# One transpose moved from DMA to TensorE, and one mask copy split and moved, in a block-sparse attention + gated MLP kernel

## The chip, the cores and the metric

The kernel runs on one core of a Trainium2 chip. A core has five engines that run at the same time, each with its own instruction queue: TensorE (PE, matrix products; its weight loads are listed as PEld), VectorE (DVE), ScalarE (ACT), GpSimd (POOL) and SyncE (SP), which here issues DMA transfers. The metric is the device time of one execution in microseconds (us).

## The reference

Inputs are q, k and v of shape (4, 8, 768, 64): batch, heads, sequence, head size. The first half is attention under a block mask with blocks of 32 positions; the second is a gated MLP over the 512 features of all heads.

```python
scores = scale * np.matmul(q, k.transpose(0, 1, 3, 2))
mask = np.abs(blk_i - blk_j) <= 1                      # neighbours
mask = mask | first and last block row and column      # edges
mask[qb block, kb block] = True for kb in sampled_blocks[qb]   # 3 per block row
attn = softmax(np.where(mask, scores, -1e9))
x = (attn @ v), heads side by side                     # (4, 768, 512)

h = np.maximum(x @ w_in, 0.0)                          # (4, 768, 1024)
u, v = h[..., :512], h[..., 512:]
v_n = (v - mean(v)) / np.sqrt(var(v) + 1e-06)
v_s = np.einsum('ts,bsd->btd', w_spatial, v_n) + b_spatial[None, :, None]
out = (u * v_s) @ w_out                                # (4, 768, 512)
```

(The mask and softmax lines are told in words here; the rest is the reference's.)

## The kernel before

**Layout.** A sequence of 768 positions is 6 chunks of 128 (`NCH`). Heads go in pairs; `p` from 0 to 15 counts pairs over all batches, four per batch. The big tile `kq` holds, for each of the 8 heads of a batch, 88 partitions: 64 with the transposed keys or queries, and 24 (`MR`, one per block) with mask rows. In the key half the mask rows say which block a position is in; in the query half they hold a penalty for each block, computed once for head 0 by `mask_rows` and the same for every head. A score product over all 88 partitions so adds the mask by itself. The rows of head 0 must therefore be copied to heads 1 to 7 once, and that is what `rows(hs, cs, eng)` does (line 239, its copies at lines 242 and 244): to heads `hs`, columns `cs`. `qcols(t, n)` names `n` thirds of the query columns from third `t` on; a third (`TW`) is 256 columns.

**First batch.** While inputs arrive, batch 0 is computed in units of a head pair and a third of the queries: first pair 0, then the pairs 1 to 3 for the first third, then the pairs 1 to 3 for the second third, then all four for the last. A unit is three slots of score products (`qk_unit`, line 405), each followed by one ScalarE exponential (line 410), and some slots later three slots of products with the values (`av_unit`, line 451), the last with a normalization on VectorE (lines 433 and 434). Units start at slots 0, 3, 6, and so on: unit 4 (pair 3, first third) at slot 12, unit 5 (pair 1, second third) at slot 15, unit 6 (pair 2, second third) at slot 18.

**Slots.** The main loop goes through numbered slots. In each it issues a score product, value products, then whatever `when(slot, ...)` has listed for it, in the order of listing. The list `ROWS` lists the mask copies; they are listed ahead of the transposes `tr_rest`. `tr_first(p)` and `tr_rest(p)` transpose a pair's keys and queries on TensorE (line 267) into a PSUM bank, from which VectorE copies them into `kq` (line 214). `tr_first` of pair 3 is in slot 10, `tr_rest` of pairs 1, 2, 3 and 0 in slots 8, 11, 14 and 17. These banks come from two that take turns (`moe_tag`), which the MLP products use too. The waits between engines follow from what each instruction reads and writes.

**GpSimd** casts what arrives from HBM to bf16, in the order in which the casts are written out: of the keys, queries and values of the pairs 0 to 3 (line 134), and then the pieces of `w_in` (line 230). SP issues the loads in its own written order; a load waits until its staging buffer is free.

**Later batches** run with whole heads (`qk_full`, line 418, exponential at line 422, `av_full`, line 469), and the MLP of the batch before (class `Moe`, products at line 545) is dealt out between them, a few products a slot.

**The last batch's MLP** has no attention beside it. Its steps are `s_product(0..5)`, the spatial product of each chunk, and then `o_product(0..5)`, the output product. The end of an `s_product` is one VectorE instruction at line 613, which writes the gated chunk into `un`. The output product needs it transposed, in `gt`, and gets it by `dma_start_transpose` on SP's queue (line 623): two chunks at a time, but chunks 4 and 5 of the last batch each by itself. Output chunks leave PSUM by ScalarE (even) or VectorE (odd), lines 217 and 214, and are written to HBM by SP (line 642); the last chunk is done in two halves of 256 columns, the second of which goes out on ScalarE's queue. PSUM banks of the last batch's products come in turn from three pairs of banks: `moe`, `av` and `sc` (`moe_ps`).

Of the kernel before, what the change touches and what calls it, by code (L numbers as in the profile page):

```python
# [26 lines left out]
def kernel(  # L27
# [22 lines left out]
    NCH = S // 128  # L50
# [5 lines left out]
    NDH = DH // 128  # L56
# [29 lines left out]
    K_, Q_ = slice(0, S), slice(S, 2 * S)  # L86

    def qcols(t0, n=1):
        return slice(S + t0 * TW, S + (t0 + n) * TW)
# [4 lines left out]
    def dram(src, p, hs=slice(0, 2), cs=slice(0, NCH)):  # L94
        b, g = divmod(p, NG)
        return src[b, 2 * g + hs.start:2 * g + hs.stop].rearrange(
            "h (p c) d -> p h (c d)", c=NCH)[:, :, cs.start * D:cs.stop * D]
# [5 lines left out]
    def load(p, nm, hs=BOTH, cs=ALLC, eng=nc.sync):  # L103
        if (nm, p) not in st:
            st[nm, p] = work.tile([128, 2, S // 2], FP32, tag="st_" + nm, bufs=3, name="st_" + nm)
        eng.dma_start(out=st[nm, p][:, hs, cs.start * D:cs.stop * D],
                      in_=dram(SRC[nm], p, hs, cs))
# [4 lines left out]
    def nat0_view():  # L112
        return nat[0].rearrange("p c h d -> p (c h d)").rearrange("p (h x) -> p h x", h=2)

    def cast(p, nm, eng, hs=BOTH, cs=ALLC):
        if nm == "v":
            dst = vv[p % NVV][:, hs, cs, 0:D]
        else:
            if p not in nat:
                nat[p] = work.tile([128, 2 * NCH, 2, D], BF16, tag="nat", bufs=4, name="nat")  # L120
            c0 = 0 if nm == "k" else NCH
            dst = nat[p][:, c0 + cs.start:c0 + cs.stop].rearrange("p c h d -> p h c d")[:, hs]
        src = st[nm, p].rearrange("p h (c d) -> p h c d", d=D)[:, hs, cs]
        if p == 0 and nm != "v":
            dst = nat0_view()[:, hs, (c0 + cs.start) * D:(c0 + cs.stop) * D]
            if cs is not C45:
                dst = dst[:, 0].rearrange("p (i t d) -> p t i d", t=2, d=D)
                src = src[:, 0].rearrange("p (t i) d -> p t i d", t=2)
            else:
                dst = dst.rearrange("p h (c d) -> p h c d", d=D)  # L130
        if eng is nc.scalar:
            nc.scalar.activation(out=dst, in_=src, func=AF.Copy)
        else:
            eng.tensor_copy(out=dst, in_=src)  # L134
# [76 lines left out]
    PL, DV = nc.gpsimd, nc.vector  # L211

    def dve_copy(o, i):
        nc.vector.tensor_copy(out=o, in_=i)  # L214
# [24 lines left out]
    def rows(hs, cs, eng=nc.vector):  # L239
        src = kq[MR, 0:1, cs].to_broadcast([NB, hs.stop - hs.start, cs.stop - cs.start])  # L240
        if eng is nc.scalar:
            nc.scalar.activation(out=kq[MR, hs, cs], in_=src, func=AF.Copy)
        else:
            eng.tensor_copy(out=kq[MR, hs, cs], in_=src)  # L244
# [12 lines left out]
    def moe_tag():  # L257
        moe_tags.rotate(1)
        if moe_tags[0] in held:
            moe_tags.rotate(1)  # L260
        return moe_tags[0]

    def bank(nm="ps", tag=None):
        return psum.tile([128, 1024], BF16, tag=tag or moe_tag(), bufs=2 if tag else 1, name=nm)

    def tr(ps, c, in_):
        nc.tensor.transpose(out=ps[:, c * 128:(c + 1) * 128], in_=in_, identity=ident)  # L267
# [47 lines left out]
    load(3, "q")  # L315
    cast(3, "k", PL)
    cast(3, "q", PL)
    load(2, "v")
    load(0, "q", cs=C45)
    load(3, "v")  # L320
# [217 lines left out]
    def product(n, lhs, rhs, last, done, w=512):  # L538
        ref = {}
        out = []  # L540
        for i in range(n):
            def run(i=i):
                if i == 0:
                    ref["ps"] = moe_ps(last)
                nc.tensor.matmul(out=ref["ps"][:, 0:w], lhsT=lhs(i), rhs=rhs(i),  # L545
                                 start=(i == 0), stop=(i == n - 1))
                if i == n - 1:
                    done(ref["ps"][:, 0:w])
            out.append(run)
        return out  # L550
# [4 lines left out]
    class Moe:  # L555
# [55 lines left out]
        def s_product(self, tcc):  # L611
            def done(ps):
                nc.vector.scalar_tensor_tensor(out=self.un[:, tcc, :], in0=ps,  # L613
                                               scalar=b_col[:, tcc:tcc + 1],
                                               in1=self.un[:, tcc, :], op0=ALU.add,
                                               op1=ALU.mult)
                if self.last and tcc >= NCH - 2:
                    g0 = tcc
                elif tcc % 2 == 1:
                    g0 = tcc - 1  # L620
                else:
                    return
                nc.sync.dma_start_transpose(
                    out=self.gt[:, g0:tcc + 1].rearrange("p t c n -> p (t c) n"),
                    in_=self.un[:, g0:tcc + 1, :].rearrange("p t d -> p (t d)"))
            return product(NCH, lambda s: w_spt[:, tcc, s, :], lambda s: self.vn[:, s, :],
                           self.last, done)

        def o_product(self, tcc):
            steps = []  # L630
            osb = {}
            parts = 2 if self.last and tcc == NCH - 1 else 1
            w = DM // parts
            for i in range(parts):
                cs = slice(i * w, (i + 1) * w)

                def done(ps, i=i, cs=cs):
                    if i == 0:
                        osb["t"] = work.tile([128, DM], FP32, tag="osb", bufs=6, name="osb")
                    on_act = (tcc + i) % 2 == 0  # L640
                    (act_copy if on_act else dve_copy)(osb["t"][:, cs], ps)
                    (nc.scalar if i else nc.sync).dma_start(
                        out=out[self.b].rearrange("(p c) d -> c p d", c=NCH)[tcc][:, cs],
                        in_=osb["t"][:, cs])
                steps += product(NDH, lambda d: self.gt[:, tcc, d, :],
                                 lambda d, cs=cs: w_out_t[:, d, cs], self.last, done, w)
            return steps
# [7 lines left out]
        def rest_steps(self):  # L655
            out = []
            for tcc in range(NCH):
                out += self.s_product(tcc)
            first = out[0]
            out[0] = lambda: ([self.vn_one(True) for _ in range(NCH)], first())  # L660
            for tcc in range(NCH):
                out += self.o_product(tcc)
            return out

    queue = deque()
# [20 lines left out]
    def when(slot, *fns):  # L686
        at.setdefault(slot, []).extend(fns)

    def c(f, *a, **kw):
        return lambda: f(*a, **kw)  # L690

    K_Q0 = slice(0, S + TW)
    ROWS = [(1, 2, 8, qcols(0)), (1, 3, 4, K_), (5, 4, 6, K_), (6, 6, 8, K_), (9, 2, 8, qcols(1, 2))]
    when(0, second)
    when(1, third)
    when(2, lambda: filler(FILL3, psum.tile([128, 512], FP32, tag=moe_tag(), bufs=1, name="wps")))
    for p, sl in ((1, 4), (2, 7), (3, 10)):
        when(sl, c(tr_first, p))
    for sl, h0, h1, cs in ROWS:
        when(sl, c(rows, slice(h0, h1), cs))  # L700
# [146 lines left out]
```

## Time and profile before

| what | before |
|---|---|
| median of 3 runs | 216.38 us (216.07, 216.38, 217.03) |
| the profiled execution | 215.56 us, of which 213.8 us span from the first to the last instruction |
| mean granted TensorE clock | 0.999 of full speed |
| TensorE busy | 205.5 us (96%) |
| ScalarE busy | 170.6 us (80%) |
| VectorE busy | 132.9 us (62%) |
| GpSimd busy | 72.1 us (34%) |
| DMA | 41.83 MB, mean 196 GB/s |

The span is from one profiled execution, and every time inside it (a start, a duration, a wait) counts from the start of that span. In a timeline a row reads: start, duration, engine, line, operation, what is written `<-` what is read, shape, how many in a row, and in square brackets how long the engine stood idle before it and what ended that. In a chain a row reads: start, duration, engine, tile and line. Matmuls overlap in the pipeline, so a row of several takes less than the sum of their durations.

### The profile page before, as it was taken

Reading aid. Unit: us, or ns where it says so; the run is one execution under the profiler, and the core shown is the slowest. Engines: PE = TensorE matmul, PEld = TensorE weight load, DVE = VectorE, ACT = ScalarE, POOL = GpSimd, SP = SyncE. Lnnn points to the kernel's source line nnn. Section 1 sums busy time; section 2 is a strip of 40 time slices with the busy share of each in tenths; the row PEclk is TensorE's granted clock in tenths of the full one; section 3 lists DMA queues with packets and bytes.
Section 4 is the critical chain, followed back from the end, with each engine's and each line's share of the span. In section 5 each row is a group of like instructions: output and inputs, shape, how many; then the busy total and the mean of one; then the engine's idle time right before and its main releaser. Section 6 shows DMA issues by size and latency. Waiting matters only on the chain.

```text
span 213.8 us, 5290 instructions
## 1 busy us (share of the span) xinstructions
PE 205.5 (96%) x2147; PEld 130.2 (61%) x2147; DVE 132.9 (62%) x286; ACT 170.6 (80%) x226; POOL 72.1 (34%) x118
## 2 busy tenths in 40 slices
PE   8897999999999999999999999999999999999991
PEld 7686878766666666656556655665565565544431
DVE  7899585979554534494986454385874443486540
ACT  6997999999999999979998888979989776275021
POOL 6886669885681412223351040131020000022000
PEclk9999999999999999999999999999999999999999
DMA  5998899999999989899491597894101225500266
GB/s 155 351 373 307 257 339 284 274 229 326 277 362 193 259 268 256 267 308 212 112 224 37 62 316 154 217 317 85 37 3 37 49 52 135 220 29 0 51 148 247
DMA packets 63324, 41.83 MB, mean 196 GB/s; under 512 B 45124, under 2 KB 58052, under 8 KB 63300
## 3 DMA queue, kind: packets, MB, share of 16 engines
q1 hardware_dynamic: 62868, 41.11, 73.9%
q10 hardware_dynamic: 432, 0.39, 0.6%
q8 instruction: 17, 0.28, 0.5%
q14 instruction: 7, 0.06, 0.1%
HBM read 24.38 MB, written 6.29 MB: 143 GB/s over the span
## 4 chain that ended last, share of the span: by engine, by line
PE 89%; DVE 6%; DMA 2%; ACT 1%; issue 0%; DVEq 0%; ACTq 0%
PE ps_moe L545 33%; PE ps L418 22%; PE ps_av L469 13%; PE ps_t L545 6%; PE ps L405 5%; PE ps_av L451 3%; PE ps_sc L545 3%; DVE kq L214 3%; DVE kq L244 2%; DMA gt<-un 2%; PE wps L182 2%; PE ps_av L267 1%; DVE xn L434 1%; ACT osb L217 0%; PE ps L267 0%
## 5 line engine op out<-in xcount | busy, mean ns | idle before, releaser
L422 ACT ACTIVATE a_all<-ps 128x768 bf16<-128x768 f32 x144 | 113.9, 812 | 15.1 <-PE ps L418 7.6
L418 PE MATMUL ps<-kq 88*128 88x384 bf16 x288 | 70.5, 325 | 0.1
L469 PEld LDWEIGHTS <-a_all 128*128 128x128 bf16 x864 | 46.5, 97 | 20.0
L469 PE MATMUL ps_av<-vv,a_all 128*128 128x65 bf16 x864 | 51.2, 194 | 0.0
L418 PEld LDWEIGHTS <-kq 88*128 88x128 bf16 x288 | 28.0, 98 | 31.0 <-issue 0.9
L545 PE MATMUL ps_moe<-w_in_t,xt 128*128 128x512 bf16 x144 | 44.0, 378 | 0.1
L410 ACT ACTIVATE a_all<-ps 128x1024 bf16<-128x1024 f32 x36 | 34.8, 1026 | 2.8 <-PE ps L405 2.6
L545 PE MATMUL ps_moe<-vn,w_spt 128*128 128x512 bf16 x108 | 32.7, 378 | 0.0
L134 POOL CAST nat<-st_k 128x768 bf16<-128x768 f32 (+2 forms) x17 | 13.5, 796 | 42.6 <-DMA st_k<-in_k_dram 42.4
L433 DVE RECIPROCAL rc<-ps_av 128x6 f32<-128x6 f32 (+1 forms) x36 | 6.6, 184 | 29.3 <-PE ps_av L469 27.8
L405 PE MATMUL ps<-kq 88*128 88x256 bf16 (+1 forms) x140 | 21.5, 275 | 2.3 <-DVE kq L214 1.5
L582 POOL TENSOR_SCALAR std<-mv 128x3 f32<-128x3 f32 (+1 forms) x9 | 2.1, 238 | 63.6 <-DVE mv L579 47.5
L613 DVE SCALAR_TENSOR_TENSOR un<-ps_moe,b_col,un 128x512 bf16<-128x512 f32 x18 | 13.5, 749 | 16.2 <-PE ps_moe L545 15.7
L545 PE MATMUL ps_moe<-w_out_t,gt 128*128 128x512 bf16 x72 | 21.5, 378 | 0.0
L545 PEld LDWEIGHTS <-xt 128*128 128x128 bf16 x192 | 15.4, 97 | 7.3 <-issue 0.3
L434 DVE TENSOR_TENSOR xn<-ps_av,rc 128x384 bf16<-128x384 f32 (+1 forms) x36 | 18.5, 513 | 1.2
L578 DVE BATCH_NORM_STATS2 stats<-vn 128x6 f32<-128x512 bf16 x24 | 16.5, 687 | 1.4 <-ACT vn L573 0.9
L405 PEld LDWEIGHTS <-kq 88*128 88x128 bf16 x140 | 12.6, 97 | 6.2 <-DVE kq L214 2.3
L134 POOL CAST nat<-st_q 128x768 bf16<-128x768 f32 (+1 forms) x18 | 14.1, 782 | 5.9 <-DMA st_q<-in_q_dram 5.3
L214 DVE COPY kq<-tt 64x1536 bf16<-64x1536 bf16 x24 | 15.9, 660 | 0.3
L134 POOL CAST vv<-st_v 128x768 bf16<-128x768 f32 x16 | 13.8, 863 | 5.6 <-DMA st_v<-in_v_dram 5.5
L451 PE MATMUL ps_av<-vv,a_all 128*128 128x65 bf16 x288 | 14.8, 194 | 0.0
(81 smaller groups left out, 209.8 us busy)
## 6 DMA issues: line engine op xcount, KB each, us to landing
st_v<-in_v_dram SPq DMA_DIRECT2D x16, 384.0 KB, 5.8
out_dram<-osb SPq DMA_DIRECT2D x23, 256.0 KB, 3.1
st_k<-in_k_dram SPq DMA_DIRECT2D x15, 384.0 KB, 4.5
st_q<-in_q_dram SPq DMA_DIRECT2D x15, 384.0 KB, 5.1
ws_f<-in_moe_w_spatial_dram SPq DMA_DIRECT2D x6, 384.0 KB, 7.2
w_f<-in_moe_w_in_dram SPq DMA_DIRECT2D x8, 256.0 KB, 7.2
w_f<-in_moe_w_out_dram SPq DMA_DIRECT2D x4, 256.0 KB, 4.2
st_q<-in_q_dram SPq DMA_DIRECT2D x2, 128.0 KB, 4.8
```

The lines of the kernel that those rows point to most:

```text
L134: eng.tensor_copy(out=dst, in_=src)
L214: nc.vector.tensor_copy(out=o, in_=i)
L405: nc.tensor.matmul(out=ps[:, at:at + n * TW], lhsT=kq[:, h, ci * 128:(ci + 1) * 128], rhs=kq[:, h, qcols(t0, n)], start=True, stop=True)
L410: nc.scalar.activation(out=out, in_=ps, func=AF.Exp, scale=0.125)
L418: nc.tensor.matmul(out=ps[:, hf * 512:hf * 512 + HALF], lhsT=kq[:, j % H, ci * 128:(ci + 1) * 128], rhs=kq[:, j % H, S + hf * HALF:S + (hf ...
L422: nc.scalar.activation(out=a_ref["h", j][:, ci, :].rearrange("p (b c) -> p b c", b=2), in_=ps.rearrange("p (b c) -> p b c", b=2)[:, :, 0:H ...
L434: nc.vector.tensor_tensor(out=out, in0=ps[:, :, 0:D], in1=rc[:, 0:n].to_broadcast([128, n, D]), op=ALU.mult)
L451: nc.tensor.matmul(out=av_ref[u][:, to, :], lhsT=a_ref[u][:, at:at + 128], rhs=vv[pp % NVV][:, h, ci, :], start=(ci == 0), stop=(ci == NCH ...
L469: nc.tensor.matmul(out=av_ref[j][:, qc, :], lhsT=a_ref["h", j][:, ci, qc * 128:(qc + 1) * 128], rhs=vv[p % NVV][:, h, ci, :], start=(ci == ...
L545: nc.tensor.matmul(out=ref["ps"][:, 0:w], lhsT=lhs(i), rhs=rhs(i), start=(i == 0), stop=(i == n - 1))
L578: nc.vector.bn_stats(out=stats, in_=self.vn[:, tcc, :])
L613: nc.vector.scalar_tensor_tensor(out=self.un[:, tcc, :], in0=ps, scalar=b_col[:, tcc:tcc + 1], in1=self.un[:, tcc, :], op0=ALU.add, op1=AL ...
```

## The change

Three edits.

1. The mask rows of the second and third query third (`qcols(1, 2)`, 512 columns) of heads 2 to 7 were copied in slot 9 by VectorE in one instruction. Now heads 4 to 7 are copied by VectorE in slot 14, and
2. heads 2 and 3 by GpSimd, in its written-out sequence right after the casts of pair 3's keys and queries.
3. Chunk 5 of the last batch, the last gated one, is no longer transposed by DMA. A step put behind `o_product(1)` transposes its four 128x128 pieces on TensorE into a PSUM bank of the `av` pair, and VectorE copies them to `gt`.

```diff
     cast(3, "k", PL)
     cast(3, "q", PL)
+    rows(slice(2, 4), qcols(1, 2), PL)
     load(2, "v")
...
-                if self.last and tcc >= NCH - 2:
+                if self.last and tcc == NCH - 1:
+                    return
+                if self.last and tcc == NCH - 2:
                     g0 = tcc
                 elif tcc % 2 == 1:
                     g0 = tcc - 1
...
+        def g_transpose(self):
+            ps = bank("ps_g", "av")
+            for d in range(NDH):
+                tr(ps, d, self.un[:, NCH - 1, d * 128:(d + 1) * 128])
+            dve_copy(self.gt[:, NCH - 1].rearrange("p c n -> p (c n)"), ps[:, 0:NDH * 128])
...
             for tcc in range(NCH):
                 out += self.o_product(tcc)
+                if self.last and tcc == 1:
+                    out.append(self.g_transpose)
             return out
...
-    ROWS = [(1, 2, 8, qcols(0)), (1, 3, 4, K_), (5, 4, 6, K_), (6, 6, 8, K_), (9, 2, 8, qcols(1, 2))]
+    ROWS = [(1, 2, 8, qcols(0)), (1, 3, 4, K_), (5, 4, 6, K_), (6, 6, 8, K_), (14, 4, 8, qcols(1, 2))]
```

## The prediction

> **What bounds the kernel now.** I read the page first: its shares, then the chain that ended last, then that chain in two windows, then the timelines of the engines there.
>
> ```profile
> PE 205.5 (96%) x2147; PEld 130.2 (61%) x2147; DVE 132.9 (62%) x286; ACT 170.6 (80%) x226; POOL 72.1 (34%) x118
> ```
>
> TensorE (PE) is busy 96% of 213.8 us, so time can only come out of its few holes or its own work. The chain of waits gives two holes. In order of time, from 15 us:
>
> ```profile
> 15.46 0.43 DVE kq L214
> 15.89 0.03 issue
> 15.92 1.43 DVE kq L244
> 17.35 0.03 issue
> 17.38 0.19 DVE rc L433
> 17.58 0.02 issue
> 17.60 0.42 DVE xn L434
> 18.02 0.60 DVE kq L214
> 18.62 0.05 issue
> 18.67 0.61 PE ps L405 x4
> ```
>
> From 7.46 to 18.62 us the chain runs on VectorE alone. Line 244 at 15.92 is the slot-9 mask copy. Around it the timeline shows the price on the other engines:
>
> ```profile
> 15.71 0.83 POOL L134 CAST vv<-st_v 128x768 bf16<-128x768 f32 x1 [0.27 <-DMA st_v<-in_v_dram]
> 15.99 0.61 PE L267 MATMUL ps<-ident,nat 128*128 128x128 bf16 x8
> 17.13 0.38 PE L267 MATMUL ps<-ident,nat 128*128 128x128 bf16 x4
> 18.48 0.83 POOL L134 CAST vv<-st_v 128x768 bf16<-128x768 f32 x1 [1.93 <-DMA st_v<-in_v_dram]
> 18.67 0.61 PE L405 MATMUL ps<-kq 88*128 88x256 bf16 x4 [1.16 <-DVE kq L214]
> 19.38 1.94 ACT L410 ACTIVATE a_all<-ps 128x1024 bf16<-128x1024 f32 x2 [1.29 <-PE ps L405]
> ```
>
> TensorE stands 1.16 us and ScalarE 1.29 us: the longest such stop. Pair 3's keys were transposed by 16.60, but their copy stood behind the mask copy and a normalization. The end of the chain:
>
> ```profile
> 203.65 1.30 PE ps_t L545 x7
> 204.95 3.96 DMA gt<-un
> 208.90 0.05 issue
> 208.95 0.61 PE ps_sc L545 x4
> ```
>
> The last output chunk waits for its DMA transpose, issued at 204.95 and landed at 208.90; TensorE had nothing else after 208.27.
>
> **Slot 9 without its copy.** Removed: one 24x3072 copy, 1.43 us. What is late next? The reciprocal follows the start of its 8 matmuls by 0.45 us (21.52 to 21.97, 24.37 to 24.82); here they start at 15.47, so it can start at 15.92, where VectorE is now free. The multiply ends at 16.56. The key copy then waits for the transposes (16.60) and starts at 16.65; at 0.69 us (64x1024) it ends at 17.34, and TensorE starts at 17.39 instead of 18.67: **1.28 us**. TensorE's last work before is four transposes from 17.13, of which the chain elsewhere charges 0.22 us for four. ScalarE ends its third exponential at 18.10 and starts 0.71 us after the scores (18.67 to 19.38), so at 18.10: no new bound. Ends: all of 1.43 above; below, nothing, if the lead is lost later.
>
> **The part moved to GpSimd.** Two heads of 512 columns, 24x1024. GpSimd's copies of this kind took 394 ns for 256 columns and 821 for 768, so 0.83 ns a column: 1.03 us, from 15.45 (end of the pair-3 query cast) to 16.48. Behind it in its queue are the value casts of pairs 2 and 3 and the w_in casts, and behind those, on SP's queue, the last two w_in loads, issued at 20.23 and 20.79, and pair 4's loads. Pair 2's cast moves to 16.5 to 17.3; its first reader is the second half of the 16 matmuls at 19.12, or 18.1 after the shift. Pair 3's cast waited 1.93 us for data and stays at 18.48, so nothing beyond it moves. Cost nothing; if the cover failed, up to 1.03 us.
>
> Do GpSimd and VectorE disturb one another? VectorE's SBUF-to-SBUF copies say yes: 24x1536 took 0.54 us alone and 1.02 from 8.47, with a cast running until 9.08; 24x3072 from 15.92 ended 0.81 us after the cast's end at 16.54. That fits waiting out the cast, then 0.26 ns a column. But copies out of PSUM (64x1024) kept to 685 ns throughout, GpSimd busy or not, and all that VectorE does from 15.92 to 17.34 reads PSUM. So I charge nothing. The Trainium skill speaks against the move: its page "Perfetto Trace Analysis", section "Optimizing Scalar/DVE Operations", warns that work shifted between these two might not help, since they share a port under an exclusive lock. Were PSUM readers locked out too, an estimate from that rule, VectorE would start at 16.48 instead of 15.92 and the early gain would be 0.72 us; the rows decide otherwise.
>
> **The part moved to slot 14.** Four heads, 24x2048, on VectorE. Alone: 0.54 + 512 x 0.26 ns = 0.68 us. It falls among seven w_in casts (19.59 to 23.87, 0.61 each). A 64x1536 copy at 38.19, in a run of such casts, took 1.00 us against 0.52 alone, so one cast is waited out: between 0.68 and 1.29, I take 1.15. It starts at 22.53 - 1.28 = 21.25 and ends at 22.40. Behind it are the two query copies of pair 3 (0.42 each, to 23.24), which free the PSUM bank that TensorE wants for pair 0's last queries at 24.62 - 1.28 = 23.34. It must end by 22.45: cost nothing by a margin of 0.05 us, at most 0.1. An xt copy wanted at 22.85 becomes 0.4 late; its bank is asked for at 23.89. Idle stretches of 0.76, 0.40 and 0.69 us take up the rest.
>
> **Does the lead of 1.28 us last?** Against it stand things that come at fixed times. Slot 15's first MLP matmul (22.69, then 21.41) needs a cast done at 20.2. The first rstd (35.74) is asked for at 37.40, then 36.12. The second comes at 48.07, behind casts fed by DMA; the vn step that uses it was at 48.26 and would be ready at 46.98, so VectorE idles 1.1 us. What it does next, v4's eviction at 50.01 to 50.70, must free a bank that TensorE wants at 52.24, then 50.96: 0.26 to spare. VectorE has holes of 0.48 and 1.75 us after 54 and catches up. I carry 1.28.
>
> **The tail.** Removed: one DMA transpose, 1.22 us of SP's queue (204.95 to 206.17) and a wait of 0.68 us on TensorE. Added after output chunk 1: four transposes, which wait for the last gating (203.76 + 0.75 = 204.51, done before TensorE gets there at 205.38), and one VectorE copy. Row: transposes of 219 ns, but 0.22 us for four back to back. Chunk 2 so starts at 205.60 instead of 205.50 (it waited for its own DMA till then anyway), chunks 2 to 4 take 0.86 + 1.73, and the last product starts at 208.19 instead of 208.95: **0.76 us**. Ends: 0.86 with the transposes free; unoverlapped, 4 x 0.22 = 0.88, it is 0.10. The VectorE copy stands behind chunk 1's eviction (205.42 + 0.69 = 206.11); 128x512 bf16 from PSUM took 414 ns, so 206.53, before chunk 3's eviction at 207.54 and well before 208.19. SP, free 1.3 us earlier, sends chunk 0 at 205.3 instead of 206.26, so no backlog. The last write leaves ScalarE's queue 0.76 earlier and lands 2.2 us on as now; I take off 0.02 for chunk 4's write close before it: 0.74.
>
> The Trainium skill's page "VectorE: DVE Perf Modes", section "The three transpose paths", gives 390 ns for a TensorE transpose of this size. By an estimate from that, four take 1.56 us, the last product starts at 209.53, and the tail loses 0.58 us; the row of four in 0.22 us is nearer.
>
> **Sum.** 1.28 + 0.74 = 2.02 us. The profiled execution took 215.56 us (span 213.8 and 1.76 around it), so 213.54; the median of the runs shown is 0.82 above the profiled one, so 216.38 - 2.02 = 214.4.
>
> **Rivals.**
> - *The lead is lost to supply.* One of the fixed times above (the 0.26 us margin at 50.7 is the closest) holds TensorE, and the tail alone counts: 216.38 - 0.74 = 215.6. For it: the DMA row of the page reads 8 or 9 tenths in nearly every slice until 42 us. Against: in that stretch no matmul waits for a DMA.
> - *The tail gains nothing.* The transposes do not overlap, or the writes end where they did: 216.38 - 1.28 = 215.1. For it: 4 x 0.22 leaves 0.10. Against: 36 such transposes overlapped.
> - *Slower: slot 14's copy is starved.* If VectorE gets the port only after the whole series of casts, the last of which ends at 25.47, the copy ends at 26.0, 3.57 us past its 22.45, and TensorE stands that long for its bank: 216.38 - 2.02 + 3.57 = 217.9. It decides from an end at 24.47 on. Against: the copy at 38.19 got in after one cast.
>
> **How the numbers follow.** Forecast 0.65, supply 0.17, tail 0.13, starved 0.05. A measurement here can tell about 0.5% (1.1 us), so faster means under 215.3: all of the forecast, three quarters of the tail case, a fifth of supply: 0.78. Slower 0.05, within 0.17. Range: the three runs spread over 1 us, so 0.4 around values between a gain of 2.29 (1.43 + 0.86) and the supply case: 213.7 to 216.0.
>
> **What would show it.** No line-244 copy on VectorE at slot 9, and the scores of slot 12 about 17.4 without their 1.16 us wait; a GpSimd copy of 1.0 us from 15.5; the slot-14 copy at 0.7 to 1.3 us and no TensorE wait at pair 0's last transposes; every later landmark some 1.3 us early, at 60, 120 and 200 us; no DMA in the chain at the end, the last product following chunk 4 directly. Landmarks back at their old times by 60 us prove me wrong, and so does a gap before the last product.

## The result, and the profile after

The changed kernel took 214.54 us (median of 8 runs, 213.62 to 215.21) against 216.28 us of the kernel before (8 runs, 215.50 to 218.01) measured beside it. The ratio is 0.9919, 95% interval 0.9892 to 0.9947: a gain of 1.7 us where 2.0 had been worked out, and a time 0.1 us above the 214.4 forecast.

The profiled execution of after is the longest of its eight (215.21 us, span 213.4), only 0.35 us shorter than the profiled one of before. Read alone, this pair would say that nearly nothing happened. The shares of the page:

```profile
PE 206.6 (97%) x2151; PEld 130.9 (61%) x2151; DVE 131.9 (62%) x287; ACT 171.0 (80%) x226; POOL 72.9 (34%) x119
```

The instruction counts are those of the edit (four more on TensorE, one more each on VectorE and GpSimd), and TensorE's busy time went up by 1.1 us. That rise is of this execution and not of the kernel: another profile of it (d3, below) has 205.3 us. The start, from the timelines of TensorE, GpSimd and VectorE of after:

```profile
10.80 0.29 PE L267 MATMUL ps<-ident,nat 128*128 128x128 bf16 x2 [0.94 <-POOL nat L134]
...
12.29 1.04 PE L406 MATMUL ps<-kq 88*128 88x256 bf16 x4
...
17.07 1.03 POOL L244 COPY kq<-kq 24x1024 bf16<-24x1024 bf16 x1
...
19.18 0.61 PE L406 MATMUL ps<-kq 88*128 88x256 bf16 x4
...
23.15 0.84 DVE L244 COPY kq<-kq 24x2048 bf16<-24x2048 bf16 x1
```

The slot-9 copy is gone and the GpSimd copy is there, yet slot 12's scores (19.18) start later than before (18.67). Two things delayed this execution. By the first line, TensorE stood 0.94 us ahead of 10.80 for a cast of GpSimd, which waited for pair 1's queries. Their load was issued at 3.04 us (3.06 before), but landed at 9.87 us, where in the profile of before it landed at 8.15. By the second line, a score group took 1.04 us that takes 0.61 elsewhere: right after that stop the granted TensorE clock fell to 0.50, from 10.96 us on, for 3.4 us. The page shows it as a 6 in the third of its 40 slices (10.7 to 16.0 us):

```profile
PEclk9969999999999999999999999999999999999999
```

From the scores behind those transposes (10.93 here, 9.84 in d3) to slot 12's scores it took 8.25 us, and in d3 7.61 with a wait of 0.47 among them, so the clock cost some 1.1 us. Neither delay comes from an edited instruction, of which the first here is the GpSimd copy at 17.07, and together they cost this one execution more than the early edit saved. The scores of slot 12 themselves follow their work with no wait.

The end, from the chain of waits of after:

```profile
205.72 0.22 PE ps_g L267 x4
205.94 1.00 PE ps_sc L546 x4
206.94 1.73 PE ps_t L546 x8
208.67 0.44 PE ps_sc L546 x4
```

The DMA of 3.96 us has left the chain. Four transposes (`ps_g`) stand in it with 0.22 us, and the last product follows chunk 4 without a gap.

The later runs profile both kernels again, and the parts of the change alone. One table serves for all; every time is in us from the start of the span, from the timelines and the transfers' landings. "Slot 13" is the start of the second score group of that unit (the one after slot 12's), "mid" that of the 37th group of score products, "chunk 0" and "last" those of the first output chunk's and the last output product.

| kernel (its profiled execution) | pair 1's queries landed | slot 13 | mid | chunk 0 | last | span |
|---|---|---|---|---|---|---|
| before | 8.15 | 19.63 | 43.57 | 203.49 | 208.95 | 213.8 |
| before, again (a3) | 9.18 | 19.82 | 43.76 | 203.51 | 209.23 | 214.1 |
| tail edit alone (a1) | 9.72 | 20.84 | 44.78 | 204.80 | 209.36 | 214.4 |
| mask edits alone (a2) | 9.36 | 19.17 | 43.11 | 202.86 | 208.40 | 213.2 |
| after | 9.87 | 20.14 | 44.08 | 203.83 | 208.51 | 213.4 |
| after, again (a4) | 8.52 | 19.42 | 43.36 | 203.18 | 207.79 | 212.8 |
| after, third (d3) | 8.38 | 18.41 | 42.41 | 202.16 | 206.85 | 212.1 |

The pair to compare is before and d3, whose loads of pair 1's queries landed within 0.25 us of one another: d3 leads by 1.22 us at slot 13, 1.16 at mid, 1.33 at chunk 0, 2.10 at the last product, 1.66 at the end.

### The profile page after: what moved, and what is told of

It reads as the page before. It is cut to its first block, busy times and chain, and to the rows that moved or that the text cites. A ratio compares the mean times of both kernels' runs of the same rounds, so it can differ in the third digit from the quotient of the medians.

```text
span 213.4 us, 5299 instructions
## 1 busy us (share of the span) xinstructions
PE 206.6 (97%) x2151; PEld 130.9 (61%) x2151; DVE 131.9 (62%) x287; ACT 171.0 (80%) x226; POOL 72.9 (34%) x119
## 4 chain that ended last, share of the span: by engine, by line
PE 92%; DMA 3%; SPq 1%; ACT 1%; POOL 0%; DVE 0%; issue 0%; ACTq 0%
PE ps_moe L546 33%; PE ps L419 22%; PE ps_av L470 13%; PE ps_t L546 7%; PE ps L406 7%; PE ps_av L452 4%; PE ps_sc L546 4%; DMA st_q<-in_q_dram 3%; PE ps L267 1%; SPq L106 1%; PE ps_av L267 1%; ACT osb L217 0%; POOL nat L134 0%; ACT a_all L423 0%; DVE xn L435 0%
## 5 line engine op out<-in xcount | busy, mean ns | idle before, releaser
L470 PEld LDWEIGHTS <-a_all 128*128 128x128 bf16 x864 | 46.5, 97 | 20.0
L470 PE MATMUL ps_av<-vv,a_all 128*128 128x65 bf16 x864 | 51.2, 194 | 0.0
L406 PE MATMUL ps<-kq 88*128 88x256 bf16 (+1 forms) x140 | 22.9, 286 | 0.7 <-ACT a_all L411 0.7
L452 PEld LDWEIGHTS <-a_all 128*128 128x128 bf16 x288 | 14.2, 100 | 2.0 <-issue 0.7
L214 DVE COPY kq<-tt 64x1536 bf16<-64x1536 bf16 x24 | 15.0, 627 | 0.3
(84 smaller groups left out, 211.8 us busy)
```

Of the source, the lines that this page charges most:

```text
L406: nc.tensor.matmul(out=ps[:, at:at + n * TW], lhsT=kq[:, h, ci * 128:(ci + 1) * 128], rhs=kq[:, h, qcols(t0, n)], start=True, stop=True)
L452: nc.tensor.matmul(out=av_ref[u][:, to, :], lhsT=a_ref[u][:, at:at + 128], rhs=vv[pp % NVV][:, h, ci, :], start=(ci == 0), stop=(ci == NCH ...
L470: nc.tensor.matmul(out=av_ref[j][:, qc, :], lhsT=a_ref["h", j][:, ci, qc * 128:(qc + 1) * 128], rhs=vv[p % NVV][:, h, ci, :], start=(ci == ...
```

## The experiments

Ratios are to the kernel before, measured beside each kernel, with 95% intervals.

### The two halves alone (a1, a2)

a1, the tail edit alone: the changed kernel with the mask copy put back.

```diff
-    rows(slice(2, 4), qcols(1, 2), PL)
-    ROWS = [..., (14, 4, 8, qcols(1, 2))]
+    ROWS = [..., (9, 2, 8, qcols(1, 2))]
```

> The kernel before with the TensorE transposes of the last gated chunk alone; the mask copies stay as they were. My theory (two parts that add up): 0.74 us less than before, a ratio of 0.9966; the last product follows chunk 4's directly, with no DMA in the end of the chain, and the 1.43 us mask copy at slot 9 with TensorE's wait of about 1.2 us is still there. Rival (the transposes or the writes eat the gain): within 0.2 us of before. Rival (the tail gives all of the change's gain, the early lead is lost on the way): 1.7 us less, 0.992.

a2, the mask edits alone: the kernel before with the first two edits.

```diff
     cast(3, "q", PL)
+    rows(slice(2, 4), qcols(1, 2), PL)
...
-    ROWS = [..., (9, 2, 8, qcols(1, 2))]
+    ROWS = [..., (14, 4, 8, qcols(1, 2))]
```

> The kernel before with the two moves of the mask copies alone (heads 2 and 3 on GpSimd, heads 4 to 7 on VectorE in slot 14); the last chunk goes by DMA as before. My theory: 1.28 us less than before, 0.994; TensorE's wait at slot 12 is gone, and from there to the last product every landmark is 1.2 to 1.3 us earlier, counted from the arrival of pair 1's queries. Rival (lead lost by 60 us to casts and loads that come at fixed times): within 0.3 us of before.

Measured: a1 215.59 us, ratio 0.9955 (0.9930 to 0.9980), so 0.97 us off 216.2 (0.43 to 1.5); a2 215.05 us, ratio 0.9953 (0.9922 to 0.9984), so 1.02 us (0.35 to 1.7). Both halves work, and they add up: 1.99 us together, against 1.7 to 2.1 for the three timings of the whole change. The chain's end in a2 still has the DMA:

```profile
204.32 4.03 DMA gt<-un
208.35 0.04 issue
208.40 0.61 PE ps_sc L546 x4
```

while a1's has the four transposes and no DMA:

```profile
206.69 0.22 PE ps_g L267 x4
206.91 0.89 PE ps_sc L545 x4
207.80 1.73 PE ps_t L545 x8
209.52 0.44 PE ps_sc L545 x4
```

From chunk 0 to the last product it is 5.46, 5.72 and 5.54 us with the DMA (before, a3, a2: mean 5.57) and 4.56, 4.68, 4.61 and 4.69 without (a1, after, a4, d3: mean 4.63): 0.94 us.

### The same two kernels again (a3, a4, d3)

a3 is the kernel before, a4 and d3 are the changed kernel, each unedited.

> The kernel before against itself, for the noise of a comparison and for a second profile of its first 20 us. Expected ratio 1.000 within 0.004. The profile of the changed kernel had the queries of pair 1 land 1.7 us later than that of before with the same issue time. If arrival sets an execution's time, this execution's span differs from 213.8 us by as much as the landing of pair 1's keys and queries and the wait on it differ; if arrival is covered, the span stays within 0.3 us of 213.8 whatever the landing.

> The changed kernel once more, for a second profile. Expected time ratio 0.991 to 0.993 (2.02 us by my sum, 1.74 by the medians measured). Its first profile spans 213.4 us with pair 1's queries landing at 9.87 us and TensorE waiting 0.94 us there. If the late landing alone made that execution long, one with a landing near 8.2 us spans 211.8 to 212.0 and has slot 12's scores at 17.4 us; if the change itself delays the landing, this one lands late again.

> The changed kernel a third time, beside the two others. Expected ratio to before 0.990 to 0.993; in the profile the time from output chunk 0 to the last product 4.6 to 4.7 us as in its two earlier profiles, and the slot-14 copy at 0.7 to 1.3 us with no TensorE wait behind it.

Measured: a3 0.9983 (0.9952 to 1.0013), which takes in 1 as it should; a4 214.38 us, 0.9901 (0.9864 to 0.9938); d3 214.33 us, 0.9912 (0.9882 to 0.9943). a3's queries landed 1.03 us later than in before, and its span is only 0.3 us longer: of the two outcomes named, the one in which the arrival is mostly covered. a4 missed what was expected of an early landing: its queries landed at 8.52, but it spans 212.8 us and not 211.8 to 212.0, so the landing alone does not set the time. The timelines of d3 (TensorE, GpSimd, VectorE) are those that the prediction drew, within 0.2 us:

```profile
14.41 0.61 PE L406 MATMUL ps<-kq 88*128 88x256 bf16 x4 [0.47 <-DVE kq L214]
...
15.65 1.03 POOL L244 COPY kq<-kq 24x1024 bf16<-24x1024 bf16 x1
...
17.45 0.61 PE L406 MATMUL ps<-kq 88*128 88x256 bf16 x4
...
21.43 1.16 DVE L244 COPY kq<-kq 24x2048 bf16<-24x2048 bf16 x1
```

Slot 12's scores start at 17.45 without a wait. The first line is a wait that before had only with 0.16 us, ahead of slot 9; a4 has more of it, and its VectorE timeline shows where it is from:

```profile
12.18 1.91 DVE L244 COPY kq<-kq 24x1536 bf16<-24x1536 bf16 x2
...
15.41 0.61 PE L406 MATMUL ps<-kq 88*128 88x256 bf16 x4 [1.00 <-DVE kq L214]
```

These are the two mask copies that stayed on VectorE, in slots 5 and 6. Alone they take some 0.55 us each; by where GpSimd's casts fall they took 1.16 us (before), 1.65 (d3), 1.67 (a3), 1.91 (a4) for the pair, and TensorE's wait ahead of slot 9 was 0.16, 0.47, 0.47 and 1.00. So a wait ahead of the edited stretch comes and goes with the arrival of the inputs, in both kernels alike.

The kernel before shows the same. With its loads landing later (a3), the slot-9 copy cost TensorE 0.68 us instead of 1.16 (timelines of VectorE, GpSimd and TensorE):

```profile
16.59 0.95 DVE L244 COPY kq<-kq 24x3072 bf16<-24x3072 bf16 x1
...
16.59 1.64 POOL L134 CAST vv<-st_v 128x768 bf16<-128x768 f32 x1 [0.24 <-DMA st_v<-in_v_dram]
...
18.86 0.61 PE L405 MATMUL ps<-kq 88*128 88x256 bf16 x4 [0.68 <-DVE kq L214]
```

and in a1 the copy cost nothing at all, because there a cast of pair 3 came later still (GpSimd waited for its DMA until 17.77) and was the last thing to wait for:

```profile
18.82 0.29 PE L267 MATMUL ps<-ident,nat 128*128 128x128 bf16 x2 [1.12 <-POOL nat L134]
```

What follows: the early edit is worth 1.2 us where the loads land early (before against d3), and less where they land late: 0.65 at slot 13 between a3 and a2, which landed at 9.18 and 9.36. At mid, the three profiles with the old mask copy (before, a3, a1) average 44.04, the four with the new ones (after, a4, d3, a2) 43.24: 0.8 us over a mix of arrivals, or 1.1 without after (42.96), which the halved clock held up.

### The copy at slot 14, made larger (b2)

Nothing on GpSimd, all six heads at slot 14 on VectorE.

```diff
-    rows(slice(2, 4), qcols(1, 2), PL)
-    ROWS = [..., (14, 4, 8, qcols(1, 2))]
+    ROWS = [..., (14, 2, 8, qcols(1, 2))]
```

> The changed kernel with all six heads' mask rows on VectorE in slot 14 and nothing on GpSimd. Slot 15's scores (pair 1, second third) need the rows of heads 2 and 3, and TensorE asks for them about 0.6 us before the copy can start (21.8 against 22.4 in the second profile of the changed kernel); the copy takes 0.95 alone and up to 1.56 with a cast waited out. My theory: TensorE waits 1.5 to 2.2 us in front of slot 15 and the whole early gain is gone: ratio to before 0.996 to 1.000. Rival (GpSimd's part does not matter, taking the copy out of slot 9 is all): as the changed kernel, 0.991.

Measured: 216.46 us, ratio 1.0035 (1.0004 to 1.0067). The timelines of VectorE and TensorE:

```profile
21.71 1.29 DVE L244 COPY kq<-kq 24x3072 bf16<-24x3072 bf16 x1
...
23.05 0.61 PE L405 MATMUL ps<-kq 88*128 88x256 bf16 x4 [1.83 <-DVE kq L244]
```

TensorE stands 1.83 us: slot 15 is unit 5, pair 1 (heads 2 and 3) in the second third of the queries, and it now needs rows that VectorE writes just then. This shows what the split is for. Heads 2 and 3 are read first, so their rows have to come from somewhere earlier, and GpSimd is where that is free; the other four can wait for slot 14. The early gain (slot 13 at 18.69) is lost here and more: b2 keeps the tail's edit, so had it lost the early gain alone it would stand at a1's 0.9955. It is 1.7 us above that, and above the 0.996 to 1.000 expected. In its profile mid comes at 45.73, some 2 us later than in before and a3. From slot 13 to mid it takes 3.0 us longer than d3 (27.04 against 24.00): 1.83 of them are this wait, 0.50 a wait at 42.09 for another VectorE copy, and the rest was not followed up.

### All six heads on GpSimd (b1)

```diff
-    rows(slice(2, 4), qcols(1, 2), PL)
+    rows(slice(2, 8), qcols(1, 2), PL)
-    ROWS = [..., (14, 4, 8, qcols(1, 2))]
+    ROWS = [...]
```

> The changed kernel with all six heads' mask rows (24x3072) copied by GpSimd and nothing in slot 14. At 0.83 ns a column the copy takes 2.7 us instead of 1.03, so the value cast of pair 2 behind it moves 1.7 us on and ends at 19.4 to 20.6 us, while slot 12's value products ask for it at 19.2 to 19.9. My theory (the split keeps the casts behind it in time): TensorE waits 0.2 to 0.8 us for that cast at slot 12, and the kernel is that much slower than the changed one, ratio to before 0.993 to 0.996. Rival (GpSimd's share is free at any size): as the changed kernel, 0.991.

Measured: 215.08 us, ratio 0.9964 (0.9942 to 0.9986). That is 0.0045 to 0.0063 above the changed kernel's three ratios, or 1.0 to 1.4 us (the medians themselves, which were not all taken side by side, differ by 0.5 to 0.8). The timelines of TensorE and GpSimd:

```profile
15.51 0.61 PE L406 MATMUL ps<-kq 88*128 88x256 bf16 x4 [1.16 <-DVE kq L214]
...
15.87 2.74 POOL L244 COPY kq<-kq 24x3072 bf16<-24x3072 bf16 x1
18.68 1.59 POOL L134 CAST vv<-st_v 128x768 bf16<-128x768 f32 x2
...
19.00 0.97 PE L452 MATMUL ps_av<-vv,a_all 128*128 128x65 bf16 x16
```

The long copy delays pair 2's value cast to 18.68, and the 16 value products that read it are stretched from the 0.68 us of d3 to 0.97, with a wait of 0.13 us where 0.2 to 0.8 had been expected. But two slots later the 0.25 us that TensorE waits for a normalization in the other kernels (at 19.74 in d3) is not there, so the loss is absorbed: from slot 12's scores to mid it takes 24.90 us, as in after (24.90) and d3 (24.96). The wait of 1.16 us ahead of slot 9 lies before the copy and is of the kind seen in a4. From chunk 0 to the end of the span it takes 10.03 us, 0.1 to 0.5 more than in the changed kernel's profiles, which no part of this edit explains. So this profile does not show where the timed loss is made; that stays open.

### The transposes without their cover (b4)

`g_transpose` ahead of `o_product(0)` instead of behind `o_product(1)`.

```diff
+            if self.last:
+                out.append(self.g_transpose)
             for tcc in range(NCH):
                 out += self.o_product(tcc)
-                if self.last and tcc == 1:
-                    out.append(self.g_transpose)
```

> The changed kernel with the TensorE transposes of the last gated chunk placed ahead of output chunk 0 instead of behind chunk 1. My theory (the two output chunks are what hides the gating of the last chunk): TensorE waits for the gating, about 0.9 us after the last spatial product, less the 0.1 us wait that it then has no more at chunk 2; 0.8 us slower than the changed kernel, ratio to before 0.994 to 0.996. Rival (the place does not matter, since the writes to HBM set the end): as the changed kernel, 0.991.

Measured: 214.91 us, ratio 0.9954 (0.9930 to 0.9978). The timeline of TensorE:

```profile
204.04 0.40 PE L267 MATMUL ps_g<-ident,un 128*128 128x128 bf16 x4 [0.92 <-DVE un L614]
```

TensorE waits for the last gating, which takes 0.75 us on VectorE, and the four transposes then cost 0.40 us in the chain instead of 0.22. The ratio is that of a2, the mask edits alone: the tail's gain is gone. So the two output chunks ahead of the transposes are what makes them nearly free.

### What is next in the start (c3, d1, d2)

If the mask copies in slots 5 and 6 collide with casts, moving one away should give more. In c3 the key rows of heads 6 and 7 (slot 6) go to GpSimd, in the place where the change had put heads 2 and 3, which go behind pair 3's value cast.

```diff
     cast(3, "q", PL)
-    rows(slice(2, 4), qcols(1, 2), PL)
+    rows(slice(6, 8), K_, PL)
...
     cast(3, "v", PL)
+    rows(slice(2, 4), qcols(1, 2), PL)
...
-    ROWS = [..., (5, 4, 6, K_), (6, 6, 8, K_), (14, 4, 8, qcols(1, 2))]
+    ROWS = [..., (5, 4, 6, K_), (14, 4, 8, qcols(1, 2))]
```

> The changed kernel with one more copy taken off VectorE: the key mask rows of heads 6 and 7 (24x1536, slot 6) go to GpSimd behind pair 3's query cast, and the small one of heads 2 and 3 behind pair 3's value cast. In the profiles VectorE worked without a break from 8.6 us to slot 12 and its two copies in slots 5 and 6 took 1.65 to 1.9 us together, where 1.1 would do alone, because each waits out a cast. My theory (VectorE's unbroken work up to slot 12 is still what holds the start): TensorE's waits for kq at slots 8 and 9 (1.4 us in the second profile of the changed kernel, 0.5 in that of the moved rows alone, none in the first) shrink by 0.5 to 0.9 us, and the kernel is 0.3 to 0.8 us faster than the changed one, ratio to before 0.987 to 0.990. Rival (arrival of the inputs holds the start now): no difference from the changed kernel within 0.2%. It would be slower if pair 2's value cast, now 1.46 us behind the query cast, comes after 19.2.

Measured: 214.87 us, ratio 0.9936 (0.9911 to 0.9962), so not faster than the change, where 0.987 to 0.990 had been expected. TensorE's idle time from 3 to 45 us fell to 0.84 us (2.51 before, 1.58 in d3), and mid came at 42.49 although the queries landed at 8.79. But from mid to the 61st score group, some 20 us on, it took 21.04 us where every kernel but d1 took 20.12 or 20.13. The timelines of GpSimd, VectorE and TensorE in that stretch:

```profile
44.39 3.55 POOL L520 CAST ws_b<-ws_f 128x256 bf16<-128x256 f32 x6 [1.93 <-DMA w_spt<-ws_b]
...
48.33 0.73 POOL L586 TENSOR_TENSOR rstd<-std,mhalf 128x2 f32<-128x2 f32 x1
49.10 0.41 DVE L188 TENSOR_SCALAR vn<-vn,mv,rstd 128x512 bf16<-128x512 bf16 x1 [1.82 <-POOL rstd L586]
...
52.08 0.38 PE L547 MATMUL ps_moe<-w_in_t,xt 128*128 128x512 bf16 x1 [0.75 <-DVE vn L188]
```

This is the prediction's closest margin, crossed. `rstd` is the factor of the normalization that GpSimd works out for VectorE. The second one stands behind casts that waited 1.93 us for a DMA; VectorE waits 1.82 us for it and so empties a PSUM bank of the MLP late, and TensorE waits 0.75 us for that bank. Of c3's lead 0.9 us are given back by the 61st group. Two kernels tried to move the obstacle: d1 is c3, d2 the changed kernel, both with the last spatial-weight casts later.

```diff
-    for i, (ld, ca) in enumerate([..., (23, 27), (23, 29)]):
+    for i, (ld, ca) in enumerate([..., (23, 38), (23, 41)]):
-    for i, sl in enumerate((23, 27, 31)):
+    for i, sl in enumerate((23, 27, 44)):
```

> The kernel with pair 3's key mask rows on GpSimd (c3) and, besides, the last six casts of w_spatial moved behind the normalization steps and pair 6's casts in GpSimd's queue (slots 38 and 41 instead of 27 and 29, their transpose to slot 44). In c3 the lead of 0.9 us over the changed kernel at slot 37 was gone by 63 us: VectorE stood 1.82 us for the second rstd, which came at 49.07 behind those casts, and TensorE 0.75 us for a bank that VectorE freed late. My theory (that rstd, at a fixed time, is what takes a further lead away): with it early, no TensorE wait at 52 us, the lead of about 0.9 us at slot 37 is still there at 63 us and at the last product, ratio to before 0.986 to 0.990. Rival (the next supply, pair 6's transpose or the casts now later, takes the lead as well): ratio as c3, 0.9936, with a new wait between 50 and 64 us.

> The changed kernel with the same move of the casts of w_spatial and nothing else. My theory (in the changed kernel the wait for the rstd costs VectorE time alone, 0.6 us and less, and no TensorE time): TensorE's landmarks between slot 37 and the last product as in the changed kernel, ratio to before within 0.002 of the changed kernel's in the same set of runs. Rival (the change's own lead is cut there already): 0.003 to 0.005 less than the changed kernel.

Measured: d1 215.85 us, ratio 0.9966 (0.9937 to 0.9995), runs from 213.71 to 220.41; d2 215.02 us, ratio 0.9944 (0.9922 to 0.9966), by point values 0.7 us slower than d3 beside it. The ratios are 0.0032 apart, more than the 0.002 expected and like the rival's 0.003 to 0.005, but their intervals overlap, so neither is decided. In d2's profile mid to the 61st group is 20.13 us, as in the changed kernel, and chunk 0 to the end 10.35 us. The profiled execution of d1 took 218.43 us, far above its median, so only its order of events is read here. The timelines of GpSimd, VectorE and TensorE of d1:

```profile
52.91 3.56 POOL L520 CAST ws_b<-ws_f 128x256 bf16<-128x256 f32 x6
...
57.62 1.73 DVE L188 TENSOR_SCALAR vn<-vn,mv,rstd 128x512 bf16<-128x512 bf16 x2 [4.40 <-POOL rstd L586]
...
58.57 0.38 PE L547 MATMUL ps_moe<-vn,w_spt 128*128 128x512 bf16 x1 [0.53 <-DVE vn L188]
```

The wait at 52 us is gone, and the moved casts now stand ahead of the third `rstd`: TensorE waits 0.53 us at 58.57 instead, and from mid to the 61st group it takes 20.91 us. The wait was moved, not removed. d2 shows the same for VectorE (3.46 us at 57.91) without a wait of TensorE there. No version tried was faster than the changed kernel. Whether leaving heads 4 to 7 in slot 9, with heads 2 and 3 on GpSimd, would do as well was not measured.

## Why the prediction was right, point by point

- **Slot 9 without its copy.** Slot 12's scores were put at 17.39 and came at 17.45 (d3), 1.22 us early against 1.28. What was not foreseen is that 1.28 is the price at an early arrival only. The profile of before that it was read from has the earliest landing of all (8.15 us; the others 8.38 to 9.87). The timed gain of this half, 1.0 us, is the better figure for the term.
- **The part on GpSimd.** 1.03 us was worked out, 1.03 measured in every profile that has it. Nothing that reads the casts behind it waited for them (in a2, after, a4 and d3 TensorE's rows have no such wait), and what VectorE read from PSUM beside it was not slowed: in d3, where it ran from 15.65 to 16.68, the reciprocal at 16.01 and the multiply at 16.23 took 0.18 and 0.42 us as everywhere. The trace so decides against the loss of 0.56 us that the exclusive lock would have made had it covered PSUM readers.
- **The part in slot 14.** 1.15 us was taken; it took 1.16 (d3), 1.11 (a4), 0.84 (after) and 0.73 (a2). The margin of 0.05 us was used up in d3: the copy ended at 22.59, the query copies behind it at 23.46, and pair 0's last transposes started at 23.51, 0.36 us after the start of the value products ahead of them, where before it was 0.25 (24.37 to 24.62). So it cost 0.1 us there, the "at most 0.1" of the prediction, and none in after and a2. b2 shows another limit, which the prediction did not work out: with heads 2 and 3 in that copy it is slot 15's scores that wait.
- **The lead lasts.** From mid to the 61st group it is 20.12 or 20.13 us in before, a1, a2, a3, after, a4 and d3. VectorE's wait for the second `rstd` was to be 1.1 us and was 0.60 (after) and 0.54 (d3); TensorE did not wait. c3 shows that the margin was real.
- **The tail.** The transposes cost 0.22 us in the chain, as read from the rows of before. The last product came 0.94 us nearer to chunk 0, against 0.76, in good part since the old landing was not always 3.96 us (4.03 in a2, 4.21 in a3). But the step "no backlog, the last write lands 2.2 us on as now" failed. From chunk 0 to the end of the span it is 10.30, 10.55 and 10.31 us with the DMA (before, a3, a2: mean 10.39) and 9.64, 9.58, 9.67 and 9.97 without (a1, after, a4, d3: mean 9.72): 0.67 us, not 0.94. The five other profiles with this tail are no better (b2 9.86, c3 9.88, d1 9.96, b1 10.03, d2 10.35); over all nine the mean is 9.88, which leaves 0.5 us. The rest went into the writes, a term that the sum had put at 0.02. The last one took 2.2 us from issue to landing in the kernel before and 2.6 in d3, by the DMA issues of before and then of d3:

```profile
out_dram<-osb ACTq DMA_DIRECT2D x1, 128.0 KB, 2.2
```

```profile
out_dram<-osb ACTq DMA_DIRECT2D x1, 128.0 KB, 2.6
```

In d3 output chunk 1 was issued at 204.80 and landed only at 208.51. Chunk 2 landed 0.63 us after it, chunk 4 1.93, and the two halves of chunk 5 followed within 0.6: here each write landed behind the one before it, so that a late chunk 1 was handed on to the end. Why it took 3.7 us is not settled. In after, a1 and a4 it took 3.3 to 3.4; in c3, b1 and d2 chunk 0's write was the late one, with 3.9 to 4.5. In b4, where the first write was issued only after the last DMA transpose had landed, neither took over 2.7. That points to the transpose still under way, but no run varied that alone.
- **The sum.** For the mask edits 1.28 us were predicted and 1.02 timed, for the tail 0.74 and 0.97: each is off by about 0.25 and in opposite directions. That the total (1.99 against 2.02) is better than its terms is luck. Each timed half has an interval of half a microsecond or more to either side, so the terms are confirmed in sign, and in size only to that; the 0.67 us of the profiles' tail lies inside it.
- **The rivals.** Supply did not hold TensorE (no wait at 50 to 52 us in after, a4 or d3) until c3 enlarged the lead. The tail gained, though part went as its rival said, by the writes. The copy in slot 14 was not starved: it took 1.16 us at most in the kernels that have it as the change made it.

## What to carry to other kernels

Where a copy holds up the bottleneck engine, ask which part of it is read first: in the split here the rows read first went early to an engine with room, and the others to a later slot. All on VectorE in the later slot did worse by a wait that the trace shows; all on GpSimd did worse by the timing, for a reason not found. A price read from one profile holds for the arrival of the inputs in that execution, so profile the same kernel again before trusting a landmark to less than a microsecond. And behind a removed wait look for two things that come at a fixed time, here a scalar from another engine at 48 us and the drain of the output writes, since they set how much of a lead is kept.

## What the runs showed of the hardware

- The load of pair 1's queries, issued at 3.04 to 3.06 us every time, landed between 8.15 and 9.87 us over the profiles. With the collisions in slots 5 and 6, and in after the halved clock, it put slot 13 of the changed kernel anywhere from 18.41 to 20.14 us.
- VectorE's SBUF-to-SBUF copies and GpSimd's casts hold one another up in both directions. In before the cast started first (15.71) and the copy at 15.92 took 1.43 us instead of 0.95. In a3 both started at 16.59: the copy took 0.95 us and the cast 1.64 instead of 0.83. The Trainium skill's page "SBUF — State Buffer", section "SBUF: two separate sides", says that the pair of ports which VectorE and GpSimd share is held for the whole instruction by whoever starts first. The row agrees: the cast's excess of 0.81 us is nearly the copy's length. VectorE's copies out of PSUM show no such excess: 64x1024 took 0.67 to 0.69 us in all 13 profiles, with GpSimd at work beside most of them.
- Four 128x128 transposes on TensorE with their inputs ready cost 0.22 us in the chain, and 0.40 where TensorE had stood idle for their input (b4).
- The granted TensorE clock fell to 0.50 for 3.4 us twice in the first 200 us of these 13 profiles: in after from 10.96 us, just behind TensorE's stop of 0.94 us, and in d1 from 89.2 us, 1.4 us behind a stop of 1.80. Stops of 1.16 us (before) and 1.83 us (b2) were followed by none, so a stop alone does not decide it.
